# Squares of two layer norms made later: a subtraction done twice in an attention, MLP and gated-MLP kernel

## The chip, the core and the metric

The kernel runs on one core of one Trainium2 chip. The metric is the device time of one execution in microseconds. The time before is the median of three runs, 1011.96 us (1010.72 to 1015.18). A profile is one more execution, recorded by the hardware; its instructions carry start times in us from the start of the span.

## What is computed

Three layers follow each other, in float32, for 4 batch entries of 448 positions. First an attention with 12 heads of 64 and capped scores. Then a layer norm over the 768 features, an MLP with 3072 hidden units and a residual. Then a gated MLP with its own norm (not touched here).

```python
scores = cap * np.tanh(scale * np.matmul(q, k.transpose(0, 1, 3, 2)) / cap)
attn = np.exp(scores - np.max(scores, axis=-1, keepdims=True))
attn = attn / (np.sum(attn, axis=-1, keepdims=True) + 1e-09)
x = np.matmul(attn, v)                      # heads joined: (4, 448, 768)
mu = np.mean(x, axis=-1, keepdims=True)
var = np.mean((x - mu) ** 2, axis=-1, keepdims=True)
xn = (x - mu) / np.sqrt(var + 1e-06) * g_ln
x = x + np.maximum(xn @ w_ch1, 0.0) @ w_ch2
```

## The kernel before

**Layout.** Features lie on partitions, positions on the free axis, so an entry is six tiles of 128 x 448 (`xts`). Matrix products of the MLP are made of three float32r products each (high by high, high by low, low by high), so each operand tile exists as a high and a low half.

**Order.** The kernel first writes down its operations in program order, through a recorder (its line 553 stands for nearly all instructions). A planner then orders each engine's queue: TensorE keeps the program order of its groups nearly as written, and the operations of VectorE, ScalarE and the DMA queue on SyncE are sorted by due times that are counted back from the TensorE groups that need them. Buffers come from small pools (10 `hs` tiles of 128 x 448, 16 `rs` pairs, 3 `wh` weight pairs, 4 `bank` and 2 `two` tiles of PSUM). Within an engine everything runs in the order planned.

**Stages.** The attention of entries 0 and 1 comes first (`attend`, `emit_s` for scores, `emit_st` for the scores of the last 64 positions, `emit_v` for the products with the values, `emit_n` for the division by the row sums, which go through DRAM by `invert`). Then follows the first product of the MLP for entries 0 and 1 (`h_units`, the middle layer), a block of 18 matmuls per 128 hidden rows and entry (`h_unit`); the attention of entries 2 and 3 is interleaved with it. From about 505 us the second product and the rest follow, all limited by TensorE.

**The norm of entries 0 and 1.** It is folded: the MLP runs on centred rows times `g_ln`, unscaled, and the standard deviation is put on the residual instead. `ln_mean` sums the features by matmuls with a tile of ones (`feature_sum`: the sum tile is split in a high and a low half in a `wh` buffer, then two matmuls `bank<-wh,onesr`), and ScalarE writes the mean into an `hs` tile. `ln_center` makes, per feature tile `k`, `u = x - mean` (VectorE, `hs<-x,hs`), the high half `u * g` (VectorE or ScalarE, `rs<-hs,g_t`), the low half (VectorE, `rs<-hs,g_t,rs`), the square of `u` (ScalarE, `hs<-hs`) and its sum over `k` (VectorE, `hs<-hs,hs`). `ln_scale`, called behind the entry's first block in `h_units`, turns the sum of squares into the standard deviation: a `feature_sum`, a trip through DRAM, and a product with each `xts` tile.

Of the kernel before, what the change touches and what calls it, by code (L numbers as in the profile page):

```python
# [14 lines left out]
ACTF = mybir.ActivationFunctionType  # L15
# [545 lines left out]
def attn_ffn_gmlp_kernel(  # L561
# [17 lines left out]
    V, A, P, T, SP = (prog.engines[n] for n in ("V", "A", "P", "PE", "D"))  # L579
    B, H = qk.shape[0], qk.shape[1]  # L580
    KD, S = out.shape[1], out.shape[3]
# [17 lines left out]
    def slots(name, n, shape, dt, pool=const):  # L599
        return Slots(name, [pool.tile(shape, dt, name=f"{name}{i}") for i in range(n)])  # L600

    rs, hs, rcs, wr, wh, small = (
        slots(name, n, shape, dt) for (name, shape, dt), n in zip((
            ("rs", [128, 2, S], F32R), ("hs", [128, S], F32),
            ("rc", [128, 4 * S // 128], F32), ("wr", [128, DM], F32),
            ("wh", [128, 2, DM], F32R), ("small", [128, 80], F32)), COUNTS))
# [42 lines left out]
    xts = [[const.tile([128, S], F32, name=f"x{i}_{k}") for k in range(KD)] for i in range(2)]  # L649
# [8 lines left out]
    rst = [const.tile([128, S], F32, name=f"rstd{i}") for i in range(2)]  # L658
# [4 lines left out]
    def f(t):  # L663
        return t.bitcast(F32)

    def sub(o, a, b, engines=None):

        with prog.either():
            for e in engines or (V,):
                e.tensor_tensor(o, a, b, ALU.subtract)  # L670

    def add(o, a, b, engines=None):
        with prog.either():
            for e in engines or (V,):
                e.tensor_tensor(o, a, b, ALU.add)
# [81 lines left out]
    def weight(kind, j, home=None):  # L757
        if (kind, j) in made:
            return made.pop((kind, j))
        n = width[kind]  # L760
        t = value(kind, j, home)
        if home:
            hi, lo = (x[:, 0:n] for x in home)
        else:
            at = 16 if kind == "wv" else 0
            o = (rb[last_pass[0]] if j == 4 else rs).get()[:, :, 0:n] if kind == "ws" else wh.get()[:, :, at:at + n]
            hi, lo = o[:, 0], o[:, 1]
        cp(hi, t, (A, V) if home is None else (V, A))
        sub(lo, t, f(hi))
        if kind in ("w1", "w2", "wu", "wo"):  # L770
            hi, lo = (x.rearrange("p (k n) -> p k n", n=128) for x in (hi, lo))
        return hi, lo
# [226 lines left out]
    ln = {}  # L999
# [5 lines left out]
    def feature_sum(ps, x, pool=wh):  # L1005

        t = pool.get()[:, :, 0:S]
        cp(t[:, 0], x)
        sub(t[:, 1], x, f(t[:, 0]))
        with prog.group():  # L1010
            for j in range(2):
                T.matmul(out=ps, lhsT=onesr, rhs=t[:, j], start=(j == 0), stop=(j == 1))

    means = {}

    def ln_mean(b):
        ps = banks.get()[:, 0:S]
        feature_sum(ps, accof[b], rs if b >= 2 else wh)
        means[b] = rst[b % 2] if b >= 2 else hs.get()
        A.activation(out=means[b], in_=ps, func=ACTF.Copy, scale=1.0 / DM)  # L1020

    def ln_center(b):

        mean, sq = means.pop(b), hs.get()
        xn[b] = []
        for k in range(KD):
            u, g = hs.get(), g_t[:, k:k + 1]
            sub(u, xts[b % 2][k], mean)  # L1030
            t = rs.get()
            with prog.either():
                V.tensor_scalar(out=t[:, 0], in0=u, scalar1=g, scalar2=None, op0=ALU.mult)
                A.activation(out=t[:, 0], in_=u, func=ACTF.Copy, scale=g)
            V.scalar_tensor_tensor(out=t[:, 1], in0=u, scalar=g, in1=f(t[:, 0]), op0=ALU.mult, op1=ALU.subtract)
            xn[b].append(t)
            A.activation(out=u if k else sq, in_=u, func=ACTF.Square)
            if k:
                add(sq, sq, u)
        ln[b] = sq  # L1040

    def ln_scale(b):
        ps = banks.get()[:, 0:S]
        feature_sum(ps, ln.pop(b))
        row = hs.get()[0:1]
        V.tensor_scalar(out=row, in0=ps[0:1], scalar1=1.0 / DM, scalar2=1e-6, op0=ALU.mult, op1=ALU.add)
        var, rstd = (t[0:CT] for t in tok_t[b % 2])
        d = dram.tile([1, S], F32, name=f"var_{b}")
        SP.dma_start(out=d, in_=row)
        SP.dma_start(out=var, in_=d.rearrange("a (n c) -> (a n) c", c=NCT))  # L1050
        P.tensor_tensor(rstd, var, mhalf[0:CT, 0:NCT], ALU.pow)
        V.tensor_tensor(var, var, rstd, ALU.mult)
        std = hs.get()
        for t, o in ((var, std), (rstd, rst[b % 2])):
            d = dram.tile([1, S], F32, name=f"{'rstd' if t is rstd else 'std'}_{b}")
            SP.dma_start(out=d.rearrange("a (n c) -> (a n) c", c=NCT), in_=t)
            SP.dma_start(out=o, in_=d.partition_broadcast(128))
        for x in xts[b % 2]:
            V.tensor_tensor(x, x, std, ALU.mult)
# [3 lines left out]
    def h_unit(b, w):  # L1063
        hi, lo = w
        ps = banks.get()[:, 0:S]
        mm3(ps, [(hi[:, k], lo[:, k], x[:, 0], x[:, 1]) for k, x in enumerate(xn[b])])
        h = hx.get()
        relu(h, ps)
        return h
# [6 lines left out]
    def mixed_h(i, h11, h12, h21, h22, t1, t2, t3, t4):  # L1076

        sub(t1, h12, h11)
        sub(t2, h22, t1)
        sub(t3, h22, h12)  # L1080
        sub(t4, h21, t2)
        for n, t in ((1, h11), (3, h22), (2, h21), (5, t1), (6, t2), (7, t3), (4, t4)):
            hidden[n, i] = dram.tile([128, S], F32, name=f"h{int(last_pass[0])}_{n}_{i}")
            SP.dma_start(out=hidden[n, i], in_=t)
# [234 lines left out]
    def gmlp(bs, nxt):  # L1319
# [3 lines left out]
        for b in nxt:  # L1323
            ln_mean(b)
# [356 lines left out]
    def row(j):  # L1681

        return j // 4 * 4 + (0, 2, 1, 3)[j % 4]

    def h_units(bs):

        j0 = 0
        for m in (4, *[2] * (NF // 2 - 2)):
            w = [weight("w1", row(j0 + j)) for j in range(m)]
            mine = {}  # L1690
            for b in bs:
                for j in range(m):
                    mine[b, j] = h_unit(b, w[j])
                    if b in ln and j == 0:
                        ln_scale(b)
                    if b % 2 and j % 2:
                        h = [mine[e, i] for i in (j - 1, j) for e in bs]
                        mixed_h((j0 + j) // 2, *h, *(hx.get() for _ in range(4)))
                    yield 3 * KD
            j0 += m  # L1700
        for b in bs:
            xn.pop(b)
# [140 lines left out]
```

## Time and profile before

| | |
|---|---|
| median of three runs | 1011.96 us (1010.72 to 1015.18) |
| the profiled execution | 1010.06 us, its span 1008.3 us |
| TensorE matmul | 999.5 us busy, 99%, 5060 instructions |
| TensorE weight load | 828.4 us, 82% |
| VectorE | 868.3 us, 86%, 1472 instructions |
| ScalarE | 580.5 us, 58%, 925 instructions |
| granted TensorE clock | full (2.4 GHz) in all 40 slices |
| chain that ended last | TensorE 78%, DMA 11%, VectorE 6%, ScalarE 3% |

Names in the rows are the program's tiles, with buffer numbers left out. `es` holds scores and their exponentials, `two` and `bank` are PSUM, `qk` and `vt` the attention's inputs, `rs` the high and low halves of normed rows (and of some weights), `wh` those of weights. A timeline row gives the start, the length from the first start to the last end of the instructions merged in it, the engine, what it writes and reads, and their count. PE is TensorE, DVE VectorE, ACT ScalarE, SPq the queue of SyncE that issues the DMAs.

### The profile page before, as it was taken

Reading aid. Unit: us, or ns where it says so; the run is one execution under the profiler, and the core shown is the slowest. Engines: PE = TensorE matmul, PEld = TensorE weight load, DVE = VectorE, ACT = ScalarE, POOL = GpSimd, SP = SyncE. Lnnn points to the kernel's source line nnn. Section 1 sums busy time; section 2 is a strip of 40 time slices with the busy share of each in tenths; the row PEclk is TensorE's granted clock in tenths of the full one; section 3 lists DMA queues with packets and bytes.
Section 4 is the critical chain, followed back from the end, with each engine's and each line's share of the span. In section 5 each row is a group of like instructions: output and inputs, shape, how many; then the busy total and the mean of one; then the engine's idle time right before and its main releaser. Section 6 shows DMA issues by size and latency. Waiting matters only on the chain.

```text
span 1008.3 us, 14836 instructions
## 1 busy us (share of the span) xinstructions
PE 999.5 (99%) x5060; PEld 828.4 (82%) x5060; DVE 868.3 (86%) x1472; ACT 580.5 (58%) x925; POOL 23.0 (2%) x22
## 2 busy tenths in 40 slices
PE   9999999999999999999999999999999999999998
PEld 2332788778778899999989899999999999998987
DVE  6979898878888789999869999877788988968996
ACT  8999776776667347674335355444454542314653
POOL 0000110000000000000001200000000000000010
PEclk9999999999999999999999999999999999999999
DMA  8444779999999999998044143565699867302402
GB/s 282 136 128 146 261 262 366 357 365 356 343 368 361 362 376 323 330 405 276 26 154 141 39 138 122 176 194 191 232 330 375 291 183 233 103 22 71 128 22 110
DMA packets 124848, 229.05 MB, mean 227 GB/s; under 512 B 21170, under 2 KB 93028, under 8 KB 124772
## 3 DMA queue, kind: packets, MB, share of 16 engines
q1 hardware_dynamic: 124772, 228.10, 66.0%
q8 instruction: 40, 0.66, 0.3%
q14 instruction: 36, 0.29, 0.1%
HBM read 157.48 MB, written 70.57 MB: 226 GB/s over the span
## 4 chain that ended last, share of the span: by engine, by line
PE 78%; DMA 11%; DVE 6%; ACT 3%; issue 1%; SPq 1%; DVEq 0%; ACTq 0%
PE bank L553 51%; PE two L553 26%; DMA hs<-inv 3%; DMA w<-in_w_dram 3%; DVE es L553 2%; DMA kept_w<-wc 2%; DMA rc<-sum 1%; ACT es L553 1%; SPq L553 1%; DMA inv<-rc 1%; DVE wr L553 1%; DVE hs L553 1%; ACT hs L553 1%; DMA qk<-in_qk_dram 1%; DVE x L553 1%
## 5 line engine op out<-in xcount | busy, mean ns | idle before, releaser
L553 PE MATMUL bank<-rs,wh 128*128 128x448 f32 x1728 | 361.9, 363 | 0.3 <-ACT hs L553 0.2
L553 PEld LDWEIGHTS bank<-rs,wh 128*128 128x128 f32 x1728 | 322.8, 187 | 27.5 <-issue 4.3
L553 PE MATMUL two<-rs,wh 128*128 128x448 f32 x462 | 103.4, 362 | 0.0
L553 ACT ACTIVATE rs<-hs 128x448 fp32r<-128x448 f32 x137 | 74.6, 570 | 43.0 <-DMA hs<-h 33.2
L553 DVE TENSOR_TENSOR rs<-hs,rs 128x448 fp32r<-128x448 f32 x159 | 94.2, 618 | 1.8 <-ACT rs L553 1.4
L553 PEld LDWEIGHTS two<-rs,wh 128*128 128x128 f32 x462 | 86.6, 187 | 5.8
L553 ACT ACTIVATE es<-es,capt 128x896 f32<-128x896 f32 x72 | 73.1, 1057 | 0.0
L553 ACT ACTIVATE es<-two,qsc 128x896 f32<-128x896 f32 x62 | 60.7, 1017 | 6.8 <-PE two L553 6.6
L553 PE MATMUL bank<-es,vt 128*64 128x448 f32 x288 | 62.2, 552 | 0.0
L553 DVE TENSOR_TENSOR wh<-wr,wh 128x768 fp32r<-128x768 f32 (+2 forms) x66 | 56.3, 856 | 3.8 <-ACT wh L553 3.5
L553 ACT ACTIVATE hs<-bank 128x448 f32<-128x448 f32 x62 | 33.6, 541 | 44.6 <-PE bank L553 34.5
L553 ACT ACTIVATE wh<-wr 128x768 fp32r<-128x768 f32 (+2 forms) x50 | 38.5, 770 | 28.2 <-PE bank L553 15.3
L553 DVE TENSOR_TENSOR es<-es,es 128x896 f32<-128x896 f32 x48 | 51.9, 1081 | 1.8 <-ACT es L553 1.4
L553 PEld LDWEIGHTS bank<-es,vt 128*64 128x64 f32 x288 | 17.4, 136 | 36.9 <-issue 26.7
L553 PE MATMUL two<-qk 64*128 64x448 f32 x168 | 39.9, 580 | 2.0 <-ACT es L553 2.0
L553 ACT ACTIVATE wc<-w 128x512 f32<-128x512 f32 x36 | 24.2, 674 | 30.0 <-DMA kept_w<-wc 13.3
L553 ACT ACTIVATE rs<-x 128x448 fp32r<-128x448 f32 x32 | 18.0, 574 | 37.5 <-DVE x L553 36.1
L553 PEld LDWEIGHTS two<-qk 64*128 64x128 f32 x168 | 14.1, 190 | 27.3 <-ACT es L553 15.4
L553 PE MATMUL two<-wh,rs 128*128 128x512 f32 x144 | 34.7, 390 | 0.0
L553 PE MATMUL bank<-rx,whb 128*128 128x448 f32 x144 | 32.7, 362 | 0.0
L553 PE MATMUL two<-rx,whb 128*128 128x448 f32 x144 | 32.7, 362 | 0.0
L553 DVE TENSOR_SCALAR wc<-wc 128x512 int32<-128x512 int32 x36 | 15.2, 423 | 19.3 <-ACT wc L553 19.0
(249 smaller groups left out, 1878.9 us busy)
## 6 DMA issues: line engine op xcount, KB each, us to landing
hs<-h SPq DMA_DIRECT2D x168, 224.0 KB, 5.2
h<-hx SPq DMA_DIRECT2D x84, 224.0 KB, 5.3
w<-in_w_dram SPq DMA_DIRECT2D x24, 768.0 KB, 6.8
w<-in_w_dram SPq DMA_DIRECT2D x36, 512.0 KB, 6.4
qk<-in_qk_dram SPq DMA_DIRECT2D x24, 448.0 KB, 5.1
h<-hs SPq DMA_DIRECT2D x48, 224.0 KB, 3.7
kept_w<-wr SPq DMA_DIRECT2D x24, 384.0 KB, 7.6
kept_w<-wc SPq DMA_DIRECT2D x36, 256.0 KB, 5.3
```

What stands on the lines that cost most here:

```text
L553: fn(*(put(a) for a in args), **{k: put(a) for k, a in kw.items()})
```

## The change

The mean of entries 0 and 1 now lies in the tile `rst[b]` that later takes the reciprocal deviation, as it already did for entries 2 and 3. `ln_center` makes no squares. A new function, `ln_square`, subtracts the mean a second time, squares and sums; it is called, together with `ln_scale`, behind the entry's first block of the weight rows 12 (entry 0) and 18 (entry 1) of 24 in the middle layer, where `ln_scale` was called at row 0 before.

```diff
     def ln_mean(b):
         ps = banks.get()[:, 0:S]
         feature_sum(ps, accof[b], rs if b >= 2 else wh)
-        means[b] = rst[b % 2] if b >= 2 else hs.get()
+        means[b] = rst[b % 2]
         A.activation(out=means[b], in_=ps, func=ACTF.Copy, scale=1.0 / DM)

     def ln_center(b):
-        mean, sq = means.pop(b), hs.get()
         xn[b] = []
         for k in range(KD):
             u, g = hs.get(), g_t[:, k:k + 1]
-            sub(u, xts[b % 2][k], mean)
+            sub(u, xts[b % 2][k], means[b])
             t = rs.get()
...
             xn[b].append(t)
-            A.activation(out=u if k else sq, in_=u, func=ACTF.Square)
+
+    def ln_square(b):
+        mean, sq = means.pop(b), hs.get()
+        for k in range(KD):
+            u = hs.get() if k else sq
+            sub(u, xts[b % 2][k], mean)
+            A.activation(out=u, in_=u, func=ACTF.Square)
             if k:
                 add(sq, sq, u)
         ln[b] = sq
@@
                     mine[b, j] = h_unit(b, w[j])
-                    if b in ln and j == 0:
+                    if j0 == 12 + 6 * b and j == 0:
+                        ln_square(b)
                         ln_scale(b)
```

The planner makes of it the following, engine by engine. TensorE's queue at the end of the attention of entry 1, before (`es,vt` and `hs,vt` are products with values, `ones` row sums, `bank<-qk` the scores of the last 64 positions):

```order
L553 MATMUL bank_139<-qk_420 64x448
L553 MATMUL bank_140<-qk_420 64x448
L553 MATMUL bank_139<-qk_421 64x448
L553 MATMUL bank_140<-qk_421 64x448
L553 MATMUL bank_138<-es_416,vt_0_423 64x448 x2
L553 MATMUL bank_138<-es_414,vt_0_423 64x448 x2
L553 MATMUL two_141<-qk_420 128x448 x2
L553 MATMUL two_142<-qk_420 128x448 x2
L553 MATMUL two_141<-qk_420 128x448 x2
L553 MATMUL bank_138<-es_418,vt_0_423 64x448 x2
```

and now:

```order
L553 MATMUL bank_139<-es_416,vt_0_423 64x448 x2
L553 MATMUL bank_139<-es_414,vt_0_423 64x448 x2
L553 MATMUL two_141<-qk_420 128x448 x2
L553 MATMUL two_142<-qk_420 128x448 x2
L553 MATMUL bank_140<-qk_420 64x448
L553 MATMUL bank_138<-qk_420 64x448
L553 MATMUL bank_140<-qk_421 64x448
L553 MATMUL bank_138<-qk_421 64x448
L553 MATMUL bank_139<-es_419,vt_0_423 64x448 x2
```

The scores of the last 64 positions moved behind two groups of values and two of scores. Apart from this and the places of the `onesr` pairs, TensorE's queue is group for group the same in both programs.

ScalarE's queue in the same place, before (`hs<-hs` without `capt` are the squares, `es<-two,qsc` the tanh that frees a PSUM tile, `es<-es,capt` the exponential):

```order
L553 ACTIVATE rs_68<-hs_80,g_t 128x448
L553 ACTIVATE hs_82<-bank_137,qsc 128x448
L553 ACTIVATE hs_87<-hs_87 128x448
L553 ACTIVATE hs_79<-hs_88 128x448
L553 ACTIVATE hs_80<-hs_80 128x448
L553 ACTIVATE es_417<-es_417,capt 128x896
L553 ACTIVATE rs_70<-hs_81,g_t 128x448
L553 ACTIVATE es_416<-two_142,qsc 128x896
L553 ACTIVATE es_415<-es_415,capt 128x896
L553 ACTIVATE hs_81<-hs_81 128x448
```

and now:

```order
L553 ACTIVATE hs_80<-bank_137,qsc 128x448
L553 ACTIVATE es_417<-es_417,capt 128x896
L553 ACTIVATE es_415<-es_415,capt 128x896
L553 ACTIVATE hs_82<-bank_138,qsc 128x448
L553 ACTIVATE hs_80<-hs_80,capt 128x448
L553 ACTIVATE hs_82<-hs_82,capt 128x448
L553 ACTIVATE es_416<-two_142,qsc 128x896
L553 ACTIVATE hs_79<-bank_139 128x448
```

The squares, and some of the high halves, have gone from between the tanh and exp instructions.

TensorE's queue in the middle layer, at weight row 12, now (`rs_67` to `rs_72` are entry 0's rows, `rs_73` to `rs_78` entry 1's; `wh_94` and so on are the three weight buffers):

```order
L553 MATMUL bank_139<-rs_78,wh_94 128x448 x3
L553 MATMUL bank_138<-rs_67,wh_95 128x448 x3
L553 MATMUL bank_138<-rs_68,wh_95 128x448 x3
L553 MATMUL bank_138<-rs_69,wh_95 128x448 x3
L553 MATMUL bank_138<-rs_71,wh_95 128x448 x3
L553 MATMUL bank_138<-rs_70,wh_95 128x448 x3
L553 MATMUL bank_138<-rs_72,wh_95 128x448 x3
L553 MATMUL bank_137<-wh_96,onesr 128x448 x2
L553 MATMUL bank_140<-rs_67,wh_94 128x448 x3
```

Before, no feature sum stood here, and the block in the last row had its weights in the third buffer. Now the feature sum holds that buffer, and the last row's block uses `wh_94` again, which the first row has only just read.

## Rows read from the trace of the kernel before

**Rows 1.** The page's busy time: engine, us (share of the span), instructions.

```profile
PE 999.5 (99%) x5060; PEld 828.4 (82%) x5060; DVE 868.3 (86%) x1472; ACT 580.5 (58%) x925; POOL 23.0 (2%) x22
```

**Rows 2.** Windows: stretch, its us, busy us (instructions) of PE, PEld, DVE, ACT, POOL, clock, DMA.

```profile
50.00:75.00 25.00, 24.63 (x126) 7.93 (x122) 20.10 (x33) 23.11 (x29) 0.00 (x0) 1.00 0.46 124
75.00:100.00 25.00, 23.73 (x114) 7.30 (x112) 24.37 (x44) 24.91 (x38) 0.00 (x0) 1.00 0.46 143
350.00:400.00 50.00, 50.00 (x252) 46.86 (x251) 44.89 (x69) 27.84 (x46) 0.00 (x0) 1.00 1.03 369
```

**Rows 3.** Timeline of TensorE at the end of entry 1's attention.

```profile
79.71 0.98 PE L553 MATMUL bank<-qk 64*64 64x448 f32 x8
...
83.16 1.77 PE L553 MATMUL two<-qk 64*128 64x448 f32 x8
...
88.43 1.15 PE L553 MATMUL bank<-hs,vt 128*64 128x448 f32 x3
...
90.63 2.00 PE L553 MATMUL bank<-qk 64*64 64x448 f32 x4
92.87 0.97 PE L553 MATMUL bank<-qk 64*64 64x448 f32 x4 [0.24 <-DMA qk<-in_qk_dram]
93.77 1.72 PE L553 MATMUL bank<-es,vt 128*64 128x448 f32 x8
95.42 1.77 PE L553 MATMUL two<-qk 64*128 64x448 f32 x8
98.15 1.02 PE L553 MATMUL two<-qk 64*128 64x448 f32 x4 [0.95 <-ACT es L553]
...
99.91 0.92 PE L553 MATMUL bank<-hs,vt 128*64 128x448 f32 x4
...
101.51 3.88 PE L553 MATMUL bank<-rs,rs 128*128 128x448 f32 x18
```

**Rows 4.** Timeline of ScalarE there: squares, and the tanh before 98.15.

```profile
82.01 1.50 ACT L553 ACTIVATE hs<-hs 128x448 f32<-128x448 f32 x3
...
92.86 1.05 ACT L553 ACTIVATE hs<-hs 128x448 f32<-128x448 f32 x2
...
97.08 1.02 ACT L553 ACTIVATE es<-two,qsc 128x896 f32<-128x896 f32 x1
```

**Rows 5.** Timeline of SyncE's queue there: the broadcasts ahead of a load.

```profile
86.34 2.40 SPq L553 DMA_DIRECT2D hs<-inv  x4
88.83 0.54 SPq L553 DMA_DIRECT2D qk<-in_qk_dram  x1
```

**Rows 6.** Timeline of VectorE there: entry 0's last two low halves.

```profile
91.30 1.27 DVE L553 SCALAR_TENSOR_TENSOR rs<-hs,g_t,rs 128x448 fp32r<-128x448 f32 x2
```

**Rows 7.** Timeline of TensorE at the feature sum of entry 1's mean.

```profile
112.42 0.41 PE L553 MATMUL bank<-wh,onesr 128*128 128x448 f32 x1
113.02 0.47 PE L553 MATMUL bank<-wh,onesr 128*128 128x448 f32 x1 [0.19 <-DVE wh L553]
113.33 3.77 PE L553 MATMUL bank<-rs,wh 128*128 128x448 f32 x18
```

**Rows 8.** Groups, 75 to 135 us: form, count | busy us, mean ns | idle before.

```profile
L553 ACT ACTIVATE hs<-hs 128x448 f32<-128x448 f32 x12 | 6.4, 570 | 0.0
...
L553 DVE TENSOR_TENSOR hs<-x,hs 128x448 f32<-128x448 f32 x12 | 7.1, 616 | 0.0
...
L553 DVE TENSOR_TENSOR hs<-hs,hs 128x448 f32<-128x448 f32 x10 | 6.1, 611 | 0.0
```

**Rows 9.** Windows of 30 us ahead of the two new places (columns as in rows 2).

```profile
200.00:230.00 30.00, 30.00 (x176) 24.47 (x173) 22.68 (x36) 23.21 (x32) 0.00 (x0) 1.00 0.97 347
...
275.00:305.00 30.00, 29.78 (x174) 22.07 (x175) 24.05 (x39) 19.81 (x29) 0.00 (x0) 1.00 1.02 367
```

**Rows 10.** Groups, 200 to 310 us: the splitting of weights on VectorE and ScalarE.

```profile
L553 DVE TENSOR_TENSOR wh<-wr,wh 128x768 fp32r<-128x768 f32 x12 | 11.3, 951 | 0.7 <-ACT wh L553 0.7
...
L553 ACT ACTIVATE wh<-wr 128x768 fp32r<-128x768 f32 x11 | 9.3, 844 | 4.4 <-DVE wr L553 4.4
```

## The prediction

> **What bounds the kernel now.** I read the page's busy times first, then windows of the stretches that the change touches, then the timeline of TensorE row by row, and last the other engines' timelines at the places where TensorE's rows stand apart. The busy times say that TensorE is the engine to look at: 999.5 us of a span of 1008.3 [rows 1]. In the middle layer it runs without a gap: 252 matmuls in 50 us, one each 0.198 us [rows 2]. VectorE with 86% and ScalarE with 58% matter only where TensorE waits for them. One such place is the end of entry 1's attention: from 75 to 100 us ScalarE is busy for 24.91 of 25 us and VectorE for 24.37, and TensorE gets 114 matmuls done instead of 126 in the slice before [rows 2]. There the busy time of TensorE tells too little (23.73 of 25), since a matmul's row can be long when it waits. The reader is to see the loss in the distance between starts. Three pieces of rows 3 take longer than equal work elsewhere in the same rows:
> - 88.43 to 90.63, four products with values and four row sums: 2.20 us. The same eight, 99.91 to 101.51, take 1.60. Lost: 0.60.
> - 90.63 to 93.77, the eight matmuls of the last 64 positions: 3.14 us. The same eight at 79.71 take 0.98. Lost: 2.16. They stall first for a PSUM bank, then for a load of `qk` [rows 3], and that load was issued at 88.83, behind four broadcasts that stood waiting in the queue of SyncE [rows 5].
> - 95.42 to 98.15, eight score matmuls: 2.73 us. At 83.16 they take 1.77. Lost: 0.96. The next group waits for ScalarE's tanh, which starts only at 97.08 [rows 3, 4].
>
> Together 3.72 us. A fourth piece follows: the feature sum of entry 1's mean takes 112.42 to 113.33, 0.91 us, where two matmuls at the pace of rows 2 take 0.40, because the low half comes late from VectorE [rows 7]. That is 0.51, so 4.2 us in all in which TensorE waits near this change.
>
> Here a rule of the Trainium skill bears on the reading: in "Perfetto Trace Analysis", section Identifying the Most-Contended Engine, matmul busy time is called a poor measure for TensorE, and weight-load busy time is to be used. By matmul busy time the slice 75 to 100 could give back 1.3 us at the most; by weight loads (7.30 us against 7.93 in the slice before [rows 2]) it is 8%, or 2.0 us of 25. The start distances give more, and the measurement decides; the sum goes by them.
>
> **What the change does, part by part.**
> Removed at 75 to 128 us: twelve squares on ScalarE of 570 ns and ten sums on VectorE of 611 ns [rows 8], half of them for entry 0 before 100 us. From the starts, entry 0's three squares at 82.01 and two at 92.86 hold ScalarE for 2.5 us before the late tanh at 97.08 [rows 4], and a sixth lies between them. So the tanh can start about 2.8 us earlier, more than the 0.96 it costs. I count this loss as gone. The pairs of 88.43 were late because the exponentials of their inputs stood behind squares; the new order puts them ahead of everything that moved. Gone: 0.60.
>
> Moved: the eight matmuls of the last 64 positions stand behind two groups of values and eight score matmuls (1.65 us by 93.77 to 95.42, and 1.77) [rows 3], so TensorE asks for their banks and for `qk` 3.4 us later, and SyncE's new order issues that `qk` load ahead of the four broadcasts instead of behind their 2.40 us [rows 5]. The 3.4 us alone are more than the 2.16 lost. Gone.
>
> What is late next: the first block of the middle layer (101.51 now) would start at 101.51 - 3.72 = 97.8. It reads six high and low pairs. The last of them stands ready at 92.6 now [rows 6]. In the new order of VectorE nine more instructions, net, stand ahead of it: sums of exponentials and divisions of entry 1 come, three sums of squares go. Nine at 0.6 us, about the mean of rows 8, are 5.4 us, so it is ready near 98.0. The block asks for its sixth pair only after 15 matmuls, at 97.8 + 3.0 = 100.8. Cover: 2.8 us.
>
> At 112.4 the feature sum of the mean now stands behind four blocks instead of three. The sum it waits for is made earlier, as the sums of squares do not stand between. Gone: 0.4 of the 0.51.
>
> The two feature sums of the variances (two matmuls of 0.2 us each) go from 117 and 131 us to about 227 and 302; TensorE's work is the same. Their trip through DRAM and the six products with the deviation are needed only by the residual after 505 us, so they cost nothing on the path while that distance holds.
>
> Added in the middle layer: twelve subtractions of 616 ns, 7.4 us of VectorE. With them come the moved sums, in all 6 x 0.616 + 5 x 0.611 = 6.8 us of VectorE and 6 x 0.57 = 3.4 us of ScalarE for each entry [rows 8]. In the 30 us ahead of the two places VectorE is idle for 7.3 and 6.0 us, ScalarE for 6.8 and 10.2 [rows 9]. So it fits, barely, and the planner may send copies and relu to ScalarE. TensorE has no wait there now. And the third weight buffer: with the feature sum in it, the next weight block has to be split while one block of 18 matmuls and the sum run, 20 x 0.198 = 4.0 us. The split takes 0.84 on ScalarE and 0.95 on VectorE one after the other [rows 10], 1.8 us, and leaves 2.2 us for what stands ahead of it in the two queues. Nothing in the trace of before shows this place, so I bound its cost between 0 and 2 us at each of the two, and take 0.3 each, nearer to 0, since the exponentials ahead of the split belong to scores that end a block earlier. VectorE's queue after 720 instructions, that is the second half of the run, is the same as before, so I count nothing there.
>
> Here the skill speaks against the change: "VectorE: DVE Perf Modes", section Rules for kernel authors, says that chained VectorE work should have fewer operations. By it the twelve subtractions are a loss of 7.4 us if VectorE set the pace; by rows 2 and 9 TensorE does, and the sum charges 0.6.
>
> **Sum.** 0.60 + 2.16 + 0.96 + 0.4 = 4.1 gained, 0.6 given back: 3.5 us. The profiled execution took 1010.06 us (span 1008.3 and 1.8 around it) and would take 1006.6. The three runs have their median 1.9 us above it, so I forecast 1011.96 - 3.5 = **1008.5 us**, 0.35% less. A measurement of this kernel tells about 0.5% from no change, 5 us.
>
> **The rivals.**
> *The wait comes back in the same place.* Entry 1's division needs its row sums through DRAM: sum out, back, reciprocal, out, broadcast. In VectorE's new order two of these reciprocals and a division stand ahead of entry 0's last pair, and VectorE waits in order. For it: four broadcasts already sat waiting for such a trip [rows 5]. Against it: the cover of 2.8 us. If the trip ends some 5 us late, 2.2 us come back and the gain is 1.3: 1010.7 us.
>
> *DMA holds the pace of the middle layer.* The DMA share is 1.03 at 350 to 400 us [rows 2], so TensorE, 3.7 us ahead, could find weights missing until it has lost its lead: 1012. Against it: not one wait of TensorE there now.
>
> *Slower: VectorE gets the middle layer's pace.* Place: the 30 us before the two moved feature sums. TensorE runs in order, so a sum of squares that is late stops every block behind it. Price: idle time that is only waiting cannot be used; if half of the 6.8 us of new VectorE work finds no room at each entry, TensorE waits 2 x 3.4 = 6.8 us, and the time is 1011.96 - 4.1 + 6.8 = 1014.7. It decides from 2 us lost per place on; at the full 6.8 at both it is 1021. Against it: 7.3 and 6.0 us idle, and lead times of 28 us that the planner allows.
>
> *That the change does not do what it says* I leave out: the order shows the squares gone from 75 to 128 us, so no chance is kept for it.
>
> **How the numbers follow.** The forecast 0.62, with its own range 1005.9 (4.2 gained on the profiled execution's level) to 1010.4; the wait that comes back 0.16; DMA 0.08; VectorE's pace 0.14. The range should leave out 2 in 10: it goes from 1005.2, a little below the forecast's own, to 1013.2, which takes in the first two rivals and the cheaper half of the third. Faster by over 0.5% is below 1006.9: the lower third of the forecast, 0.22. Slower by over 0.5% is above 1017.0: the dear half of VectorE's pace, 0.07. The rest, 0.71, is within 0.5%.
>
> **What would show it.** Right: the first block `bank<-rs,rs` of 18 starts near 98 instead of 101.5; the eight matmuls of the last 64 positions take about 1 us; the slice 75 to 100 holds some 124 matmuls; `bank<-wh,onesr` pairs stand near 226 and 301 with no idle time before them; VectorE has about 12 instructions more and some 7 us more busy time; from 130 us on every block starts about 4 us earlier than before, to the end. Wrong: a gap of over 1 us before the first block, or before the pairs near 226 and 301 or the block behind them, or a lead of 4 us at 130 us that shrinks towards 505.

## The result, and the profile after

The changed kernel takes 1017.92 us (median of 12 runs, 1016.11 to 1022.93) beside 1012.09 us of the kernel before (12 runs): ratio 1.0062, 95% interval 1.0043 to 1.0081. It is slower, and the time lies outside the range. Its profiled execution took 1017.49 us, with a span of 1015.7 us. The profiled execution of the kernel before, 1010.06 us, lies some 2 us below that kernel's median, so a difference of the two traces is about 1.5 us too large.

The page's busy times answer to [rows 1]: 13 instructions and 6.5 us more on VectorE, 0.2 us more weight load on TensorE. Only VectorE's 6.5 us come near what is lost; whether they are the cause is tested below.

```profile
PE 1001.2 (99%) x5060; PEld 828.6 (82%) x5060; DVE 874.8 (86%) x1485; ACT 579.1 (57%) x924; POOL 16.6 (2%) x22
```

Windows of the changed kernel, columns as in [rows 2]:

```profile
75.00:100.00 25.00, 25.00 (x133) 10.01 (x130) 23.29 (x42) 24.67 (x34) 0.00 (x0) 1.00 0.55 156
...
150.00:350.00 200.00, 193.86 (x1061) 150.13 (x1061) 166.96 (x273) 135.04 (x201) 2.26 (x2) 0.99 1.00 344
...
310.00:320.00 10.00, 7.69 (x31) 6.71 (x31) 9.92 (x17) 6.54 (x10) 0.00 (x0) 0.83 1.00 359
```

The same 200 us in the kernel before:

```profile
150.00:350.00 200.00, 199.72 (x1106) 157.23 (x1105) 165.22 (x265) 134.82 (x194) 1.04 (x1) 1.00 1.01 359
```

Two opposite things happened. The slice 75 to 100 holds 133 matmuls instead of 114: the early gain is there. The 200 us from 150 to 350 hold 1061 instead of 1106: 45 matmuls fewer, about 9 us at 0.2 us each. The DMA engines are busy the whole time in both (share 1.00 and 1.01) and move 344 GB/s instead of 359.

TensorE's timeline of the changed kernel shows where, in order of time:

```profile
89.02 1.67 PE L553 MATMUL bank<-es,vt 128*64 128x448 f32 x8
90.62 1.77 PE L553 MATMUL two<-qk 64*128 64x448 f32 x8
92.33 0.98 PE L553 MATMUL bank<-qk 64*64 64x448 f32 x8
...
96.60 3.88 PE L553 MATMUL bank<-rs,rs 128*128 128x448 f32 x18
...
111.12 0.57 PE L553 MATMUL bank<-wh,onesr 128*128 128x448 f32 x2
...
138.89 0.89 PE L553 MATMUL bank<-rs 64*128 64x448 f32 x2 [0.99 <-ACT hs L553]
...
226.39 0.57 PE L553 MATMUL bank<-wh,onesr 128*128 128x448 f32 x2
226.79 5.51 PE L553 MATMUL bank<-rs,wh 128*128 128x448 f32 x26
...
305.02 0.56 PE L553 MATMUL bank<-wh,onesr 128*128 128x448 f32 x2
305.42 3.77 PE L553 MATMUL bank<-rs,wh 128*128 128x448 f32 x18
309.79 0.67 PE L553 MATMUL bank<-rs,wh 128*128 128x448 f32 x2 [0.59 <-ACT wh L553]
312.78 8.57 PE L553 MATMUL bank<-rs,wh 128*128 128x448 f32 x34 [2.31 <-DVE wh L553]
```

Up to 131 us all is as foreseen, and better. Row by row against [rows 3]: the eight matmuls of the last 64 positions take 0.98 us instead of 3.14, the score matmuls 1.77 instead of 2.73, the first block starts at 96.60 instead of 101.51, and the feature sum of entry 1's mean takes two matmuls' time instead of the 0.91 of [rows 7].

Part of the lead is there ahead of anything that the change touches: the eight matmuls that start at 79.71 us in [rows 3] start 0.8 us earlier here,

```profile
78.94 0.98 PE L553 MATMUL bank<-qk 64*64 64x448 f32 x8
```

Then the lead is lost. Number TensorE's matmuls in the order of its queue, without those of the feature sums. The start of a matmul in the changed kernel minus the start of the one with the same number in the kernel before shows the lead: below zero TensorE is ahead, above zero it lags. The first line is the start in the kernel before, in us:

```
start before      101.5  131.1  154.0  232.0  299.3  320.0  367.0  415.0 1000.1
lead, changed     -4.91  -6.23  -4.55  -3.24  -1.29  +5.33  +5.19  +6.25  +7.37
```

A lead of 6.2 us at 131 becomes a lag of 7.4, 13.6 us in all: 1.7 near 137, 3.3 on the way to 299, 6.6 from 299 to 320, and 2.0 later. The two moved feature sums (226.39, 305.02) do not wait, but each takes 0.4 us that stood ahead of 131 us before, so 0.8 of the 13.6 us is work in another place. The largest piece stands at the second block behind the second sum, where the high half of the weights comes 0.59 us late (309.79) and the low half another 2.31 (312.78). The engines that make those weights, ScalarE and then VectorE:

```profile
137.50 0.91 ACT L553 ACTIVATE wr<-w 128x768 f32<-128x768 f32 x1 [2.65 <-DMA w<-in_w_dram]
138.32 0.95 ACT L553 ACTIVATE hs<-bank 128x448 f32<-128x448 f32 x2
...
308.34 0.66 ACT L553 ACTIVATE wc<-w 128x512 f32<-128x512 f32 x1 [2.76 <-DMA kept_w<-wc]
308.91 0.83 ACT L553 ACTIVATE wh<-wr 128x768 fp32r<-128x768 f32 x1
```

```profile
306.26 0.62 DVE L553 TENSOR_TENSOR hs<-hs,hs 128x448 f32<-128x448 f32 x1 [1.66 <-DMA hs<-inv]
...
308.89 0.62 DVE L553 TENSOR_TENSOR hs<-hs,hs 128x448 f32<-128x448 f32 x1 [1.23 <-DMA hs<-inv]
...
311.77 0.95 DVE L553 TENSOR_TENSOR wh<-wr,wh 128x768 fp32r<-128x768 f32 x1
```

The split `wh<-wr` shows no wait of its own. It stands in ScalarE's queue behind the unpacking of a weight of the second product (`wc<-w`), which waits 2.76 us until the buffer `wc` has been written out to DRAM, and in VectorE's queue behind two divisions of entry 2's or 3's attention, which wait 1.66 and 1.23 us for broadcasts (transfers too). Near 137 it is the same: the copy out of a PSUM bank that frees TensorE's next group stands behind the unpacking of a weight (`wr<-w`) that has not landed, a wait of 2.65 us. Behind the wait of 2.31 us TensorE is also slow for a while: 34 matmuls take 8.57 us instead of 6.8, and the clock granted from 310 to 320 is 0.83 in the mean, so part of that stretch was at 1.2 GHz instead of 2.4.

One sentence ahead of the prediction has to be put right: the second product starts at about 347 us (its first change of accumulators, 21.6 us of matmuls later, is at 368), not at 505.

### The profile page after: what moved, and what is told of

It is laid out like the page before. It is cut to its first block, busy times and chain, and to the rows that moved or that the text cites. A ratio compares the mean times of both kernels' runs of the same rounds, so it can differ in the third digit from the quotient of the medians.

```text
span 1015.7 us, 14863 instructions
## 1 busy us (share of the span) xinstructions
PE 1001.2 (99%) x5060; PEld 828.6 (82%) x5060; DVE 874.8 (86%) x1485; ACT 579.1 (57%) x924; POOL 16.6 (2%) x22
## 2 busy tenths in 40 slices
DMA packets 124848, 229.05 MB, mean 226 GB/s; under 512 B 21170, under 2 KB 93028, under 8 KB 124772
## 4 chain that ended last, share of the span: by engine, by line
PE 69%; DMA 21%; DVE 4%; ACT 3%; SPq 2%; issue 1%; ACTq 0%; DVEq 0%
PE bank L553 42%; PE two L553 26%; DMA w<-in_w_dram 6%; DMA h<-hx 3%; DMA hs<-h 2%; DMA hs<-inv 2%; DMA kept_w<-wr 2%; SPq L553 2%; ACT es L553 2%; DMA kept_w<-wc 1%; DMA wqs<-kept_w 1%; DMA rc<-sum 1%; DMA inv<-rc 1%; DMA wqm<-kept_w 1%; DVE hs L553 1%
## 5 line engine op out<-in xcount | busy, mean ns | idle before, releaser
L553 ACT ACTIVATE wh<-wr 128x768 fp32r<-128x768 f32 (+2 forms) x46 | 35.1, 762 | 26.3 <-DVE wr L553 13.1
L553 PEld LDWEIGHTS two<-wh,rs 128*128 128x128 f32 x144 | 27.0, 188 | 5.5
```

Of the source, the lines that this page charges most:

```text
L553: fn(*(put(a) for a in args), **{k: put(a) for k, a in kw.items()})
```

## The experiments

**The first theories.** Three were put down. T1: the moved sum holds the third `wh` buffer, so the next weights are split too late. T2: VectorE's added work is too much there. T3: a TensorE that runs ahead meets transfers that have not landed yet, until its lead is gone.

*The sums in another pool.*

```diff
-        feature_sum(ps, ln.pop(b))
+        feature_sum(ps, ln.pop(b), rs)
```

> The changed kernel, with the high and low half of the two variance sums in an rs buffer instead of the third wh buffer; everything else is as changed. Theory T1 (the moved sum holds the third weight buffer, so that the next block is split while TensorE has only 4 us of work; the 5.9 us lost from 299 to 316 us are this): the wait for wh near 313 us and the half-clock stretch behind it are gone, about 5.9 us come back: 1017.9 - 5.9 = 1012.0, and TensorE's lead of 1.3 us over the kernel before at 299 us is still there at 320. Theory T2 (twelve more subtractions and the moved sums are too much for VectorE there, whichever buffer the sum is in): 1017 to 1018, and a loss of 4 us or more between 299 and 320 as in the changed kernel. Theory T3 (a TensorE that runs ahead in the middle layer meets loads that have not landed, so it falls back to the pace of the kernel before, and no further): about 1012 too, but the lead at 320 us is zero, lost by waits that end on a DMA or on an engine that waited for one.

1019.96 us, ratio 1.0067 (1.0047 to 1.0088). T1 falls: with the buffer free there is still a wait for `wh` of about the same size behind the second sum, and others have come. TensorE's timeline of this kernel:

```profile
244.99 12.67 PE L553 MATMUL bank<-rs,wh 128*128 128x448 f32 x54 [1.87 <-ACT hs L553]
...
308.73 0.57 PE L553 MATMUL bank<-rs,onesr 128*128 128x448 f32 x2
309.14 4.17 PE L553 MATMUL bank<-rs,wh 128*128 128x448 f32 x20
315.48 12.26 PE L553 MATMUL bank<-rs,wh 128*128 128x448 f32 x52 [2.17 <-DVE wh L553]
```

T3 as written falls too: the lead is not only eaten, this trace ends 10 us behind.

*Without the second subtraction.*

```diff
-            sub(u, xts[b % 2][k], mean)
-            A.activation(out=u, in_=u, func=ACTF.Square)
+            A.activation(out=u, in_=xts[b % 2][k], func=ACTF.Square)
```

> The changed kernel without the second subtraction: the squares are taken of the uncentred tiles, which leaves the centring out of the variance; the sums, the wh buffer and all places stay. VectorE loses twelve instructions of 616 ns, 3.7 us in each entry's stretch. T1: the buffer is held as before, so most of the 5.9 us stay lost: 1015 to 1018. T2: half or more of the added VectorE work is gone, so the loss goes with it: 1011 to 1013. T3: between, 1014 to 1017, as loads do not change.

1017.38 us, 1.0059 (1.0036 to 1.0083). T2 falls: without the twelve subtractions it is as slow. The loss only sits elsewhere, 6.3 us of it at one place: 3.18 us of waiting, and then 61 matmuls in 15.29 us instead of 12.2, at a clock of 0.81 from 350 to 360. TensorE's timeline of this kernel:

```profile
357.02 15.29 PE L553 MATMUL bank<-rs,wh 128*128 128x448 f32 x61 [3.18 <-ACT hx L553]
```

*Only the scale moved, in the kernel before.*

```diff
-                    if b in ln and j == 0:
+                    if j0 == 12 + 6 * b and j == 0:
                         ln_scale(b)
```

> The kernel before, with only the call of the scale (the variance sum, its trip and the six products) moved behind the first block of weight rows 12 and 18; squares and their sums stay early, so no VectorE work is added and nothing changes at 75 to 100 us. T1: the sum holds the third wh buffer at the same places, so a loss comes there without any added VectorE work: 2 to 6 us, 1014 to 1018. T2: no loss, 1011 to 1013. T3: no lead, so nothing to fall back from, 1011 to 1013.

1015.89 us, 1.0035 (1.0016 to 1.0053), with ten runs from 1010.40 to 1018.96. This is a loss without any added VectorE work and without the early gain. It lies in T1's range, as the moved sum holds the third buffer here too, so by itself it does not tell T1 from a cost of any new order. The profiled run is the fastest of the ten, so it shows little of the loss: one longer wait of TensorE, at 351 us,

```profile
351.47 6.88 PE L553 MATMUL bank<-rs,wh 128*128 128x448 f32 x33 [1.51 <-ACT hx L553]
```

*Entry 0 alone moved.*

```diff
-                    if j0 == 12 + 6 * b and j == 0:
+                    if j0 == (12, 0)[b] and j == 0:
```

> The changed kernel with entry 0 as changed (row 12) and the squares and scale of entry 1 behind its first block again (row 0, second subtraction kept). T1: the loss of 5.9 us at 299 to 316 is gone with the sum there, the one at entry 0's place (under 1 us) stays, and some of the 4.2 us of early gain remains unless entry 1's squares stand in the way at 113 us: 1009 to 1012. T2: the same at entry 1's place, but 3.7 us more of VectorE work at 110 to 135 us, where it is at 95%, costs 1 to 3 us: 1011 to 1014. T3: the lead is eaten by 320 us, 1012.

1017.78 us, 1.0057 (1.0036 to 1.0078). No theory foresaw this. The lead is still 4.3 us at 320 us, with nothing lost at 299 to 316, and then 12.5 us go between 355 and 415, in many waits for operands of the second product and at a granted clock of 0.83 from 360 to 370 and from 375 to 385 us. The two longest waits are

```profile
362.91 0.68 PE L553 MATMUL two<-rs,wh 128*128 128x448 f32 x2 [1.31 <-DVE rs L553]
...
378.86 4.05 PE L553 MATMUL two<-rs,wh 128*128 128x448 f32 x11 [1.36 <-DVE rs L553]
```

The changed kernel and the three variants of it tried so far lose about the same time between 131 and 415 us, at places that differ from one to the next. So the cause was to be sought in what these places share, and that is DMA engines that are busy throughout.

**Room for the transfers.** Two theories were left. D: the transfers fill the DMA engines, those that come late make the engines that wait for them late, and these pass the delay on to TensorE. Q: what the change puts into the queues of VectorE and ScalarE costs the time, and transfers only happen to be what they wait for. In both kernels 56 of the 60 raw weight loads (the expectation says 58; 22 of the 24 large and 34 of the 36 small ones) were cut to half their columns: `cut` slices the issued transfer, and the planner sees the full one, so every queue keeps its order. The other half of each such tile keeps old data. 17.6 MB of 229.05 are not moved, in as many packets as before (124848), so bytes are what is taken away. The lines of the edit that choose the loads:

```diff
-            raw = raw6[0 if n > DH else 2].get()[:, 0:n]
-            SP.dma_start(out=raw.rearrange("p n t -> p (n t)"), in_=source[kind][j].bitcast(I32))
...
+            pool = raw6[0 if n > DH else 2]
+            part = n if len(pool.bufs) >= 2 and kind in ("w1", "w2") else None
+            raw = pool.get()[:, 0:n]
+            SP.dma_start(out=raw.rearrange("p n t -> p (n t)"), in_=source[kind][j].bitcast(I32), cut=part)
```

> The kernel before, with 58 of the 60 raw weight loads of the middle layer (all but the first two of each size) cut to half their columns: 18 MB less to move between 100 and 335 us, of about 100 MB, and the order of every queue unchanged. Half of each later raw tile is old data, so the product is not the reference's. After the first four runs the theories are: D (the transfers fill the DMA engines from 150 to 400 us in both programs, so TensorE's lead of 6.2 us cannot be kept: it meets transfers that land late, and VectorE, ScalarE and SyncE, which wait for them in order, pass the delay on) and Q (the lead is lost in the queues of VectorE and ScalarE by what the change puts into them; transfers only happen to be what they wait for). This kernel is the base for its twin with the change. Both: 1008 to 1012, since TensorE has hardly a wait there before; DMA share near 0.8 instead of 1.0 from 150 to 340 us.

> The changed kernel with the same 58 loads cut to half. D: with the DMA engines no longer full the lead of 6.2 us at 125 us is kept, at least 4 us of it, and the time is 4 to 6 us below that of the kernel before with half loads: 1003 to 1008. Q: the feature sums, the buffers and the twelve subtractions are as they were, so the loss at 299 to 316 us stays, and the time is 3 to 6 us above its twin: 1012 to 1017.

Before with half loads: 1010.48 us (1008.96 to 1012.74). Changed with half loads: **1007.28 us** (1006.04 to 1007.68), 0.9950 (0.9933 to 0.9967) of the kernel before. The ranges of the two do not touch. With room for the transfers the change gains 3.2 us, beside the 3.5 of the prediction; it is 0.8 less than the least that D asked for. Q falls: sums, buffers and subtractions are all there, VectorE is busier (172.5 us instead of 167.0), and TensorE gets as many matmuls done as in the kernel before. The window of the changed kernel with half loads, and behind it TensorE's timeline at the place that had cost 6.6 us:

```profile
150.00:350.00 200.00, 199.59 (x1106) 157.16 (x1105) 172.54 (x284) 138.32 (x206) 2.37 (x2) 1.00 0.88 291
```

```profile
296.24 3.88 PE L553 MATMUL bank<-rs,wh 128*128 128x448 f32 x18
299.95 0.56 PE L553 MATMUL bank<-wh,onesr 128*128 128x448 f32 x2
300.35 10.97 PE L553 MATMUL bank<-rs,wh 128*128 128x448 f32 x54
```

54 matmuls in a row behind the second moved sum, without a gap. From 299.3 to 320 us only 0.4 us of lead are lost, which is the sum's own two matmuls, and 0.9 around the first sum (lead 5.7 us at 199, 4.8 at 232): its own 0.4, and a wait of 0.41 us for ScalarE at 217.64, ahead of it.

*Another order of the kernel before.*

```diff
-AFTER = 0.05, 0.9, 0.93
+AFTER = 0.05, 0.9, 0.931
```

> The kernel before, with one constant of the place of the attention of entries 2 and 3 in the middle layer changed from 0.93 to 0.931: the planner makes another order of the same instructions from about 200 us on, and nothing of the change is in it. D, with the addition that the order before is one in which hardly a late transfer meets TensorE, by choice or by luck: 1013 to 1019, lost between 200 and 400 us. Q: 1011 to 1013, since no work is added and no buffer taken.

1014.72 us, 1.0029 (1.0009 to 1.0049), with 3.3 us of the lag coming between 367 and 415. So an order that has nothing of the change in it, neither added work nor a held buffer, loses too, if less.

*Squares and scales at rows 4 and 8.*

```diff
-                    if j0 == 12 + 6 * b and j == 0:
+                    if j0 == 4 + 4 * b and j == 0:
```

> The changed kernel with the squares and scales behind the first blocks of weight rows 4 (entry 0) and 8 (entry 1) instead of 12 and 18; the order up to about 130 us is the same, with its 6 us of lead. D: the lead is lost in the full stretch as before, 1011 to 1018. A third theory, S (the trips of the two deviations through DRAM hold SyncE's queue at 325 to 350 us, where the DMA share fell to 0.70 in the changed kernel): the trips are now made before 220 us, the dip at 335 to 340 is gone, and 3 us or more come back: 1009 to 1014, with no loss behind 320 us.

1021.41 us, 1.0091 (1.0067 to 1.0115). S (the trips of the deviations through DRAM hold up SyncE's queue) falls: with the trips made early it is slower still, 7.8 us lost between 367 and 415. It is also above the 1011 to 1018 that D gave.

**Spreading the transfers.** All bytes moved, the second product's weights asked for in another order and later.

```diff
-AFTER = 0.05, 0.9, 0.93
+AFTER = 0.05, 0.97, 0.93
-            rows = [("w2", j) for j in range(NG * KD)]
+            rows = [("w2", g * KD + d) for ds in (range(KD // 2), range(KD // 2, KD)) for g in range(NG) for d in ds]
```

> The changed kernel, with the same weight loads asked for in another order and over a longer stretch: of the second product's weights the left halves, which its first pass needs, come first, then the right ones, which it needs some 20 us later, and the last is asked for at 0.97 of the middle layer instead of 0.90. Not a byte less is moved. D, which the half loads bore out: the DMA engines are asked for some 8% less per us between 110 and 340 us, so part of the lead of 6.2 us is kept: 1008 to 1015, below the changed kernel by 3 us or more. If the engines' own queues (Q) decided, or if any new order costs what the reshuffled kernel before cost, it stays at 1015 to 1020.

> As the run before, but from 0.03 to 1.0 of the middle layer. D: the same direction, a little further, as long as the right halves do not come too late for the second product at 347 to 370 us: 1006 to 1014. Q: 1015 to 1020.

> The changed kernel with left halves first, from 0.02 to 0.95: loads start earlier, into the stretch from 100 to 130 us where the DMA share is 0.75. D: 1008 to 1015, if SyncE's queue and the two raw buffers let them start earlier; without that, as the changed kernel, 1016 to 1019. Q: 1015 to 1020.

> The kernel before with the same order and stretch as the first of these four (left halves first, 0.05 to 0.97). D: it had no wait to lose there, so at best as the kernel before, 1010 to 1013, and at worst what a new order cost the reshuffled kernel, 1013 to 1016. Beside its twin it tells whether the change gains once the transfers have room: the twin 2 to 5 us below it.

Changed kernel: 1022.46 us, 1.0096 (1.0076 to 1.0116); from 0.03 to 1.0, 1023.06, 1.0104 (1.0074 to 1.0133); from 0.02 to 0.95, 1021.08, 1.0096 (1.0066 to 1.0125). Kernel before: 1014.67, 1.0033 (1.0020 to 1.0046). Missed: the three variants of the changed kernel are slower, not faster, and the twin of the kernel before is the faster of its pair. Asked for over a longer stretch, the transfers still fill it: in the first of them the DMA share is 0.95 to 1.02 in each 50 us from 150 to 300, and the lead is gone at 154 us already.

**Is the lead itself the loss?** Idle matmuls ahead of the first block, 24 or 48, which the planner does not count (from the edit):

```diff
         with prog.group():
...
+            if not filled:
+                filled.append(1)
+                for _ in range(24):
+                    T.matmul(out=o, lhsT=pairs[0][0], rhs=pairs[0][2], start=True, stop=True, idle=True)
```

> The changed kernel with 24 idle matmuls of 0.2 us ahead of its first middle-layer block, 4.8 us of TensorE alone, so that TensorE enters the middle layer about as late as in the kernel before; every queue's order is as changed, since the planner sees no cost in them. D: when TensorE is not 4.9 us ahead it has that much less to wait for, so the 4.8 us cost little or nothing: 1014 to 1019, beside 1017.9 without them. Less than 1016.5 would say that running ahead is a loss in itself (waits, and the half clock behind them). Q (the queues' own work sets the loss, not the lead): 1021 to 1023.

> The kernel before with the same 24 idle matmuls ahead of its first middle-layer block. D: it has only some 1 us of waits to give back, so nearly all of the 4.8 us stays: 1014 to 1017. Were TensorE free to run late at no cost there too, it would be 1011 to 1013, and the transfers would already set the time of the kernel before.

> The changed kernel with 48 idle matmuls, 9.5 us, so that TensorE enters the middle layer about 4.6 us later than in the kernel before. D: if waits for transfers are gone by then, 1012.1 + 4.6 + what the moved sums cost by themselves (0 to 3): 1016 to 1020, so within 2 us of the changed kernel with no delay. Q: 1026 to 1028.

Changed, 4.8 us later: 1020.05 us, 1.0083 (1.0064 to 1.0102), 2.1 above the changed kernel. Changed, 9.5 us later: 1025.31, 1.0132 (1.0109 to 1.0155), 7.4 above it. Before, 4.8 us later: 1015.56, 1.0038 (1.0024 to 1.0052), 3.5 above. The first is above D's bound of 1019 and under Q's 1021, the second above D's 1020 and under Q's 1026. By the medians some of a delay is absorbed (2.7 of 4.8 us, 2.1 of 9.5; the interval of the first overlaps that of the changed kernel), but the large waits come back in the same places, as TensorE's timeline of the kernel with 24 idle matmuls shows:

```profile
144.61 0.90 PE L553 MATMUL bank<-rs 64*128 64x448 f32 x2 [1.57 <-ACT hs L553]
...
307.66 3.77 PE L553 MATMUL bank<-rs,wh 128*128 128x448 f32 x18
311.99 0.68 PE L553 MATMUL bank<-rs,wh 128*128 128x448 f32 x2 [0.55 <-ACT wh L553]
314.99 8.65 PE L553 MATMUL bank<-rs,wh 128*128 128x448 f32 x34 [2.32 <-DVE wh L553]
```

2.32 us behind the second sum, where it was 2.31. So these waits do not come from running ahead. They belong to the order of the queues at full transfers. (A late TensorE delays transfers too: the GB/s from 100 to 125 us fall from 244 to 188.)

**Which bytes?** Only one kind of load cut, in the changed kernel: the second product's weights (34 loads), then the first's (22 loads). Then the second product's loads later by some 10 us, with all bytes (`AFTER` from 0.09 to 0.94). The edit of the first, against the half loads:

```diff
-            part = n if len(pool.bufs) >= 2 and kind in ("w1", "w2") else None
+            part = n if len(pool.bufs) >= 2 and kind == "w2" else None
```

> The changed kernel with only the raw loads of the second product's weights cut to half their columns (34 of 36 loads, 8.9 MB less), every queue's order as changed. Half of those tiles is old data. These weights are needed only from 347 us on, but in the changed kernel their loads are issued up to 14 us earlier than before (the 25th at 246.4 instead of 260.1 us). If all bytes count alike (D with one pool of bandwidth), this and its twin with the first product's weights cut give about the same, halfway to the half loads' 1007: 1010 to 1014. If it is these early loads that stand in the way of the others, nearly the whole gain comes here: 1007 to 1010, and the twin stays at 1014 to 1018.

> The changed kernel with only the raw loads of the first product's weights cut to half (22 of 24 loads, 8.7 MB less). All bytes alike: as its twin, 1010 to 1014. If what TensorE waits for near 137 us is the landing of these very loads, the 1.7 us lost there come back in any case: the lead of 6.2 us at 131 us is still above 5.5 at 154.

> The changed kernel with the second product's weights asked for from 0.09 to 0.94 of the middle layer instead of 0.05 to 0.90, some 10 us later, all bytes moved. If the early loads of these weights stand in the way, 1011 to 1015, a gain of 3 us or more on the changed kernel; if any new order at full transfers loses, 1016 to 1022.

1008.47 us, 0.9965 (0.9947 to 0.9982), and 1008.25 us, 0.9966 (0.9946 to 0.9986): the same, and each brings nearly the whole gain, not half of it as was expected of equal bytes. Moved later with all bytes: 1021.91 us, 1.0115 (1.0072 to 1.0158), so the early loads alone are not it: it came out as was expected if any new order at full transfers loses. The windows of the first and of the second:

```profile
150.00:350.00 200.00, 199.59 (x1106) 157.30 (x1106) 173.54 (x287) 140.35 (x208) 2.03 (x2) 1.00 0.95 323
```

```profile
150.00:350.00 200.00, 199.50 (x1104) 156.90 (x1103) 172.28 (x283) 139.00 (x206) 2.49 (x2) 1.00 0.95 326
```

For the time it does not matter which of these bytes go. With 8.9 or 8.7 MB less, some 4% of all, the DMA share is 0.95 instead of 1.00 and 45 and 43 matmuls are back. The lead through the stretch, kernel by kernel (starts in the kernel before in the first line; the delayed kernels counted without their idle matmuls; each row is one execution):

```
start before                    101.5  131.1  154.0  232.0  299.3  320.0  367.0  415.0 1000.1
changed                         -4.91  -6.23  -4.55  -3.24  -1.29  +5.33  +5.19  +6.25  +7.37
changed, sums in rs             -4.59  -4.66  -0.65  +0.24  +3.68  +9.24  +9.36  +9.36  +9.99
changed, entry 0 alone          -4.05  -5.39  -4.37  -3.97  -4.25  -4.26  +0.23  +8.25  +8.59
changed, 24 idle matmuls        +0.37  -1.08  +1.18  +2.07  +2.20  +7.62  +7.49  +7.49  +8.76
changed, half of all loads      -4.40  -5.72  -5.69  -4.81  -5.10  -4.70  -4.83  -3.91  -2.45
changed, half of second weights -4.37  -5.12  -3.15  -2.26  -2.54  -2.14  -2.27  -2.06  -0.96
changed, half of first weights  -4.88  -6.21  -6.01  -5.11  -5.40  -4.64  -4.77  -3.19  -2.11
before, half of all loads       -0.74  -1.24  -1.24  -1.24  -1.53  -1.54  -1.66  -1.66  -0.54
before, other order (0.931)     -0.61  -0.93  -0.93  -0.93  -1.22  -1.23  -0.17  +3.09  +4.18
before, 24 idle matmuls         +4.08  +3.47  +3.47  +3.47  +3.18  +3.17  +3.35  +3.36  +6.07
```

In the pair with one kind of load cut, the wait near 137 us goes only where the very loads it waits for are cut (1.97 us lost from 131 to 154 with half of the second weights, 0.20 with half of the first).

No version here beats both kernels with all bytes moved and all work done: ten were run, and the best of them, the reordered kernel before, is 0.29% slower than before.

## Why the prediction was wrong

- **The early gain: right, in size too.** Its terms made 4.1 us, and the traces show 4.9 at the first block and 6.2 at 131 us. But 0.8 of this belongs to the profiled execution of the kernel before, since TensorE is that far ahead before any of the pieces begins, and kernels whose early part is unchanged are as far ahead at 101.5 us (0.74 with half loads, 0.61 with the other order). Another 0.8 is the two feature sums that have only moved. What is left, some 4.6, is the forecast's 4.1 and little more. Between the two kernels with half loads the first block starts 3.66 us apart, beside 0.60 + 2.16 + 0.96 = 3.72. Entry 0's last pair is not late, so that rival did not come.
- **The judgement by weight loads: no guide here.** The prediction weighed the Trainium skill, "Perfetto Trace Analysis", Identifying the Most-Contended Engine, against start distances. From 75 to 100 us weight-load time rose by 37% (7.30 to 10.01 us), matmuls by 17%; over the whole span it reads 828.6 beside 828.4 us while the time rose by 6. The same section of the Trainium skill says that for DMA the share of busy time misleads, and that HBM utilization (here the moved GB/s) is to be used. Here 1.00 falls to 0.95 and 344 GB/s to 323 where the waits vanish, but the kernel before, almost without waits, stands at 1.01 and 359 GB/s, more than any version of the changed kernel moved from 150 to 350 us. So neither figure says whether TensorE will wait.
- **VectorE's added work: right.** 13 instructions and 6.5 us, where 12 and 7.4 were counted, and leaving the subtractions out changes nothing that can be told from zero (1017.38 beside 1017.92). The Trainium skill's rule on fewer operations ("VectorE: DVE Perf Modes", Rules for kernel authors) was read as a loss of 7.4 us if VectorE set the pace; it does not, so the near agreement with the measured 5.8 us is chance. The rival "VectorE gets the middle layer's pace" named time and sign rightly and the cause wrongly.
- **The step that failed** is the one on the third buffer: "bound its cost between 0 and 2 us at each of the two, and take 0.3 each". The 0.6 us given back became 13.6 in the traces, of which 0.8 is the two sums themselves. At the first place 1.0 us of lead goes between 199 and 232 us, within the bound; at the second 6.6 instead of at most 2; and some 6 us go where the sum had no term at all (1.7 near 137, 2.0 between 232 and 299, 2.0 behind 320). With transfers out of the way the two places cost 0.9 and 0.4 us, so as a count of work the term was right. But it "leaves 2.2 us for what stands ahead of it in the two queues", and only work was put into those 2.2 us. At the second place what stands ahead waits for transfers, 2.76 us on ScalarE and 2.89 on VectorE. And it is no matter of that buffer: with the sums in `rs` as much is lost. The term should have covered the whole stretch from 130 to 415 us, with every instruction there that waits for a DMA and has TensorE's work behind it.
- **The rival on DMA: right cause, wrong price.** It stood at 0.08 and 1012, "until it has lost its lead". Against it the prediction held "not one wait of TensorE there now". That was no sign of room. The order before just fits at a share of 1.03 [rows 2]: three other orders cost some 3 us with no work added (ratios 1.0029, 1.0033 and 1.0035; in the third the moved sum also holds the `wh` buffer). And the loss did not end where the lead did: a late transfer was passed on through in-order queues, and the wait of 2.31 us was followed by a clock of 0.83 over 10 us.
- **The trips through DRAM cost nothing: not disproved,** though the reason given, that the residual needs them after 505 us, was wrong: the six products of the second sum stand at 364 us. The lead does not change from 343 to 367 us.

Two things stay open. Why orders with the early part lose 14 to 20 us from 131 us on, and new orders without it only 2 to 6, is not settled; throwing the lead away absorbs 2.7 us of it, and a loss of 1 us or more between 131 and 154 us is in most of them. And which single instruction in the queues would have to move was not tried.

## What to carry to other kernels

A TensorE that never waits is no sign of room where the DMA share is 1.0. Here the order of transfers just fitted, and 4 us gained ahead of such a stretch were no gain at its end until bytes were taken out of it. Before counting on a lead, halve some loads without touching any order: if the gain appears then, transfers hold it back. When a step moves in a program whose queues are planned, charge the new order itself, some 3 us here, and look in each in-order queue for instructions that wait for a DMA ahead of what TensorE needs. And before reading a lead off two traces, look at a place ahead of the change: 0.8 us of it were there already.

## What was not expected of the hardware

- The step is steep. From 150 to 350 us the kernel before moves 359 GB/s and the changed one 344. A tenth less than the 359 (323 or 326 GB/s, with one kind of load halved) is enough for 9 to 10 us, and a fifth less (291 GB/s, with both) brings only 1 us more (1007.28 beside 1008.25 and 1008.47).
- The granted clock: after waits of 1.87 us (244.99), 2.31 (312.78) and 3.18 us (357.02), in three kernels, the next matmuls run slower, 54 in 12.67 instead of 10.8 us, 34 in 8.57 instead of 6.8, 61 in 15.29 instead of 12.2: 1.8 to 3.1 us, about as much as the wait again. The clock granted there is 0.83, 0.83 and 0.81 over 10 us, between the levels of 1.2 and 2.4 GHz. After the wait of 0.99 us at 138.89 the next 98 matmuls run at full pace (19.2 us).
